# A written order of tasks for each engine, in place of priorities, in a fused attention and gated-MLP kernel

## The chip, the cores and the metric

The kernel runs on one NeuronCore of one Trainium2 chip. The metric is the device time of one execution in microseconds (us), lower is better.

## The reference

Everything is float32. Attention over 4 batches of 8 heads, 576 tokens, head dimension 64, with a threshold below the row maximum; its output goes through two feed-forward layers. The 2304 tokens have 512 features; the layers are 1024 and 2048 wide.

```python
def _attn_ref(q, k, v, tau):
    scores = scale * np.matmul(q, k.transpose(0, 1, 3, 2))
    thresh = np.max(scores, axis=-1, keepdims=True) - tau
    scores = np.where(scores >= thresh, scores, -1000000000.0)
    ...  # softmax
    return np.matmul(attn, v)

def _moe_ref(x, w_in, w_out, g_ln):
    h = x @ w_in
    solu = h * softmax(h)
    ...  # layer norm over the features, times g_ln
    return ln @ w_out

def _moe2_ref(x, w_in, w_out):
    h = x @ w_in
    return (h * tanh(softplus(h))) @ w_out
```

## The kernel before

The program is written as 5062 tasks, each one or a few instructions of one engine with its inputs and buffers. There are 1268 tasks for TensorE (PE), 1617 for VectorE (DVE), 1268 for ScalarE (ACT), 206 for GpSimd (POOL), 695 for SyncE (SP), which issues nearly all DMAs, and 8 without an engine of this count.

**Attention** goes by pairs of heads and blocks of 128 query rows. A score tile is made by `s_tile`: TensorE writes it to a PSUM buffer `st` (two) or `s3` (L810 for the first eight pairs, which use half the array's rows at a time; L817 for the others). VectorE takes its row maximum (TENSOR_REDUCE, L823), a short scalar op (L826) makes the threshold, ScalarE takes the exp (L824), and VectorE masks and sums it (SCALAR_TENSOR_TENSOR, L827); that last step releases the score buffer. `turn` transposes the result on TensorE (L854, L857, and L859 for the sums) into a PSUM bank `p_ta` or `p_mo`, ScalarE copies it out (L835), and `pv` multiplies it with V (L904). A score tile, a transpose and a product with V use the TensorE array in different modes.

**Weights** come as 64-bit numbers and are taken apart by `convert`: ScalarE (L651, L657), VectorE (L654 or L657, L659, L660, L662) and GpSimd (L665, L668) work on them between the other tasks; the mish layer's weights get seven sums and differences (L715, `add7`) and are stored to DRAM as `w2c`.

**The gated layer** (`moe_h` L961, `layer_norm` L968 to L991, `moe_t` L1010, `moe_y` L1031) follows each batch of attention, in tiles of 128 tokens.

**The mish layer** works in five visits of 768 tokens. `ff_in` and `ff_out` compute 2x2 blocks by seven products each; a product is six matmuls of 128x384 (L1129) into a PSUM bank `hoa` or `hob`. Weights are loaded into eight buffers A (L1159) and twenty buffers B (L1155), activations into y (L1145), partial sums into `acc` (L1234); results are stored from `acc` (L1278, L1283). ScalarE copies banks (L1179), takes mish (L1185) and splits numbers (L1215); VectorE adds and subtracts (L1182, L1189, L1217, L1253).

**The order.** Before the program is emitted, the `Plan` lays out all tasks in a planned time. At each step it looks, for each engine, at the tasks whose inputs are there, and takes the one with the best priority: the recorded number of the task (`KEYS`), less 250 times the planned wait. What it takes decides the order on each engine, which buffer a task gets, and where idle TensorE time early in the program is filled with dummy matmuls (L604). On the chip each engine runs its instructions in that order, each waiting for its semaphores. SP's DMAs are such a queue too.

Of the kernel before, what the change touches and what calls it, by code (L numbers as in the profile page):

```python
# [12 lines left out]
ALU = mybir.AluOpType  # L13
# [5 lines left out]
KEYS = (  # L19
    "bghl04mzxphMsWqgBaWiSh0xdrjfBgVsaTsRaL3isQkaTX8FbzLdamXiIot2iVxjpjrcGZkWcYPWYpa2OlRjcABeIUd3bb7qRL3WGfaQydyWiEEgyCgZYeth"  # L20
    "aE1aGZdM/iTbgiOjTZcmHbFhadHdpdiIUc9ye4uT98jVSc+/aq+gsha6wd0DgWpiCNchjboygDmdLZdNkgY8cAdZHKe7jaxobONeH5iRjeDlZ5td50dFoe2F"
    "fFTeLYbAdhOednab7dbhzdomcPaejxcnedvqZ7CcrchKeesXYREiK0goIfVAhtIb55a7FTRQjKQcWCcLxgGgcJabpidFpdDgfHjfBYZiPdUhbYMeHEYAjZTk"
    "bVNbzFd9CazYhlZZ0cV8Lfe7a/udINbI+gxObNvdSvhMvbrVgKObPmbXedyte+DcPcbrQe7oZ8ldb5aGjevKZkrb2Hea9ayicRadhda7rb7YeEAaoecSjZWB"
    "Z1wYUdb7/awTUNabW5a+cWmYbTYcBxWTCbZ+VPEY2vf2/g2eX58dZ+ZECfW7bf5ZJkYltZ7NZtoWqcbs6YI0fAfYUibevYpOYcMZm+gdKah8d+0a7HaJ2cNY"
    "aqeY8edcJep7Xv3dbFXhAYjeWPWYqNYYzYh2bmbasva/YU1/fvxXtNaZuYRdcO0bYWZgYYKBX8ycwPYW2bfsXSAWlQZycUEEdA6UzubigYLbYh0ZHrYsZZs2"
    "ZDxXm0acFYCDYCJXiEYwPaZXW5HX+0X7zYUZav2V2qfYcY4eZ+MXilaPGXoJYksWuHX6xYI7Ym4ZCZXm1ZR4YKDZxLXVQaJbXrIY8eWq5ZwSYXMbM4Wp6YZv"
    "W9LXPmXQMYQyXmTaVMX4cXf/Vl6WuLVxXZImc6nbNrYN8ZscUoQX2sWzWb7kZXEZDDWGEXYQVcGaFgWhhWOrWsCZ09UL+aEPXpQWMvWTOZkvU7QSr6Z9cWc4"
    "aXzYaIZLQWeAZZqXjlYYEanTZ7UVUZVcxWF+Xh/ZozUpWYxHbeLaMPaw6W3KWp0W3ZY6Jb2IWM1VNLWE7XZoWZxZN7WZNXluZo+WxpWZmWtLWE/XxeX+/Zy6"
    "YyEX49aESX2vYU5WJoZegV29WU1YxPdDuXIPUmgW1OUeTW++Vv3WhhYh2YkBZz8VGNU9DVlZXJjXU6VSAUlyUnFXhhYqSV5+Tn1UhTXYEWYJY2RXGAUwMVCM"
    "UobOm0VoMWmwZV/XbwU34YMGVkTVUwZWbXojUTSXNxT8PT7sUJBWbaU+qUn2UR/VTlWPbT5YVqOUz4UUCXLnSGMVdvWTVWXZTwQUbeROcYAfW35UY3SwNXaN"  # L30
    "S9uWZ1WuIVG4WdJTB7VkRVMXWw0VWlWVeVT/XEbSocTeXYBxVAgTGvS95WIVTq7SLKUe1UKTWiSVQ6RUCU7SWokVSyUEKTrjTpbVfTS07X88Ud7V1LVB8W/S"
    "TfBV7dTybU9HVFDTVIWjBVyOV1LTHMTo2TqTTknUtTUpPR0wUUZUb+UKPVsLULST8kWkbTLeVHdTw3VFrUOoUFBTZxTagV7JQ1mVaOUN2TUoT9zVjDSzeSzp"
    "TF1UeBTArUspTsOYo2TDxTQdPt4TvyV7tSf7TTtTUKUErS7GTAIUP/UmYU8qUGTTUiUBVS+jYM5TfTSgJS2FS7eUg0TsZUJVU/KR9GTwaS/YSlYT1wSiPT3B"
    "S00Sf5UFBTVnVYAVwbTdHSJwSdiTSqR6zT33S21S/2TlyRdBVJCQvlSiTS2CUkxPwZTV+SpUTDFT2jUPCTcJTxhTLTT3RSTXS+vT41SmJUEnT+BSZcSfyTU7"
    "Sk3VauVv9STaSxJSeITA1TjUT0uSmUSbpS1FSZvSmtVEBQnESs+S0sSpjTGYUVkIiFApIli/GmaPSVYMubTKZsFmzbhGckT+Y16Y0dpN5fvvfi6gDgm08XiV"
    "mzOWKLlk1cTUTcBOeEb3aii1b6NW5Vm70fkudpCbO4cY2fuhbUoisVYq3aBHfMFcRyhJFcO8fESmHqnvdkkklctX/3gjxc+hgdEbGGXWpVuMpimbEXfkei/0"
    "ozzw9prYJmDQknGbQ9YFPTHOdqycgqYlCc6lbwxjfVm65dwXXBWbsFhxRiADdJxaNycjYg72hfPoHPeNgXpBhvidFzchjgdpT2igmwv8ZVFZe00lAbTgbhys"
    "iedb0mkjyUrncVOqDGexagSLouki0QejZiFecNld2NhKjgZ3nliiAkjxLfJ1faKfn9VUmmsbeJudO+XgwcALbPfds6fSGcHRc6wdb7fuseQ1gr7aKmc6Uq3d"
    "cr3bk1nPAaSbbLkpNbe1wWsXcEdXMVg73cDGljXnuqYgFhFMfRmqyKdvBc8TfB6duniLLluZey2d0iesxhoPfSdcuSZuecNaV6Bm2glPsghGebzcmxnw2a9C"
    "ewMcroeJWkBoiVbbQJbE2gTzm88h6dfvOe8taVig6ScdFhjihihhg3hQ9fY/aePluWb+1ifmeCMaOLfnZefNh61bcpdEpfFac2Djy1gGUd0HnozlPThROXzv"  # L40
    "fC4jXqfcdf5vmpqfUQlorajToIcgu3doCav8dxljgDV9ggupghsjKcbJzj9NdW5jbdegtWOheu4e5/eMZh1naGFjRoVVKjPlZPbeRTbAieNbfHAif6c+Ne1R"
    "cVvcgKePPeGMZkVgDLisjSjWc1WeLlczVaPKmJibljcARhPHilKf4AfNAVMXfpvedBZTVchzbtzeVifT8hErfCAgNxfpFdakdTEg16n07emQcvOem1WXIh7F"
# [154 lines left out]
class Plan:  # L197
# [5 lines left out]


    COLD = 60.0
    RULE = 250.0, 3.0
    ISSUE, FIRST, LATENCY = 0.48, 0.95, 1.8
    LANES = 8
    LOAD = 1.3
# [28 lines left out]
    def place(self, choose, put, first):  # L238
# [7 lines left out]
        n = 0  # L246
# [1104 lines left out]
```

## Time and profile before

| what | value |
|---|---|
| median of 3 runs | 864.36 us (863.97 to 864.73) |
| profiled execution | 865.65 us, of it 863.9 us span from first to last instruction |
| TensorE busy | 842.5 us, 98% of the span |
| VectorE busy | 754.4 us, 87% |
| ScalarE busy | 626.7 us, 73% |
| GpSimd busy | 243.5 us, 28% |

A matmul's record reaches to its modelled end and overlaps the next one's, so TensorE's busy share is more than what it needs. Busy time counts neither waits nor DMA issue. The line numbers are those of the kernel before; from L606 on, a line of the changed kernel stands 15 lines earlier.

### The profile page before, as it was taken

The page shows a single profiled execution, that of the slowest core. Times are in us where ns is not written, and L with a number is a line of the kernel's source. Part 1 is how long each engine was busy: PE and PEld are TensorE (multiplying, and loading weights), DVE is VectorE, ACT ScalarE, POOL GpSimd, SP SyncE. Part 2 cuts the span into 40 slices and gives each one's busy share as a digit, 9 for nine tenths or more (in the row PEclk, how much of TensorE's full clock was granted, in tenths as well). Part 3 has the DMA queues.
Part 4 walks back from the last instruction along what each step waited for, and adds up shares of the span by engine and source line. Part 5 has one row for each costly group of instructions (what it writes and reads, how often), then busy time and mean ns, then how long its engine had stood idle before and what let it go on. Part 6 is the DMA issues. An engine that isn't in the chain of part 4 may idle for free.

```text
span 863.9 us, 16472 instructions
## 1 busy us (share of the span) xinstructions
PE 842.5 (98%) x5432; PEld 731.9 (85%) x5433; DVE 754.4 (87%) x1782; ACT 626.7 (73%) x1308; POOL 243.5 (28%) x210
## 2 busy tenths in 40 slices
PE   8889999999999999999999999999999999999998
PEld 4455666677788888797899999999999999989998
DVE  6997999899998999898867898889999998868786
ACT  5898898889898989867556778665757665646451
POOL 2346464533444434242222211011112210000000
PEclk9999999999999999999999999999999999999999
DMA  7666544323755374647988679999999999776733
GB/s 221 185 188 206 165 150 131 121 94 112 232 152 181 118 228 127 209 144 244 365 268 241 216 225 367 348 329 334 322 320 310 321 308 355 248 275 230 233 123 92
DMA packets 158197, 195.22 MB, mean 226 GB/s; under 512 B 15376, under 2 KB 115744, under 8 KB 158112
## 3 DMA queue, kind: packets, MB, share of 16 engines
q1 hardware_dynamic: 157680, 193.91, 69.0%
q8 instruction: 43, 0.70, 0.3%
q14 instruction: 42, 0.34, 0.1%
q10 hardware_dynamic: 432, 0.26, 0.1%
HBM read 142.94 MB, written 51.19 MB: 225 GB/s over the span
## 4 chain that ended last, share of the span: by engine, by line
PE 72%; DVE 5%; DMA 4%; ACT 3%; issue 1%; POOL 1%; SPq 0%; ACTq 0%; DVEq 0%; POOLq 0%
PE hoa L1129 27%; PE hob L1129 10%; PE p_mo L1031 7%; PE p_mo L961 6%; PE p_ta L904 5%; PE p_ta L854 4%; PE st L817 4%; PE hoa L1031 3%; PE hoa L961 2%; PE st L810 2%; DVE e L827 1%; PE p_mo L1010 1%; DVE m L823 1%; DMA A<-w2c 1%; DMA y<-yc 1%
## 5 line engine op out<-in xcount | busy, mean ns | idle before, releaser
L827 DVE SCALAR_TENSOR_TENSOR e<-st,m,e 128x576 f32<-128x576 f32 x139 | 111.7, 813 | 14.3 <-ACT e L824 11.2
L1129 PE MATMUL hoa<-y,A 128*128 128x384 f32 x594 | 115.5, 336 | 1.7 <-DMA A<-w2c 1.5
L824 ACT ACTIVATE e<-st,m 128x576 f32<-128x576 f32 x139 | 101.9, 743 | 18.2 <-DVE m L823 16.8
L823 DVE TENSOR_REDUCE m<-st 128x1 f32<-128x576 f32 x139 | 102.6, 751 | 9.6 <-PE st L810 6.2
L1129 PE MATMUL hoa<-gh,B 128*128 128x384 f32 x492 | 105.7, 335 | 0.8 <-ACT B L1156 0.5
L1129 PEld LDWEIGHTS hoa<-y,A 128*128 128x128 f32 x594 | 103.4, 188 | 2.9 <-ACT gf L1185 1.8
L1215 ACT ACTIVATE gh<-gf 128x384 fp32r<-128x384 f32 x168 | 81.7, 518 | 28.9 <-PE hob L1129 8.9
L1217 DVE TENSOR_TENSOR gl<-gf,gh 128x384 fp32r<-128x384 f32 x168 | 87.0, 558 | 2.7 <-PE hob L1129 1.9
L1129 PEld LDWEIGHTS hoa<-gh,B 128*128 128x128 f32 x492 | 86.7, 188 | 2.1 <-ACT B L1156 0.8
L854 PE MATMUL p_ta<-ident,e 128*128 128x128 f32 x576 | 83.5, 277 | 4.3 <-DVE m L826 1.3
L1189 POOL TENSOR_TENSOR gf<-gf 128x384 f32<-128x384 f32 x24 | 24.5, 1019 | 218.6 <-DVE gf L1189 154.9
L854 PEld LDWEIGHTS p_ta<-ident,e 128*128 128x128 f32 x576 | 64.8, 140 | 23.3 <-issue 3.8
L665 POOL TENSOR_TENSOR ws<-cf,cl 128x512 uint32<-128x512 uint32 x32 | 41.4, 1292 | 128.0 <-DVE cf L662 20.3
L1253 DVE TENSOR_TENSOR acc<-acc,hoa 128x384 f32<-128x384 f32 x107 | 57.2, 548 | 9.4 <-PE hoa L1129 7.3
L1031 PE MATMUL p_mo<-LH,W2H 128*128 128x256 f32 x216 | 64.3, 298 | 0.0
L1185 ACT ACTIVATE gf<-gf 128x384 f32<-128x384 f32 x72 | 37.6, 523 | 36.2 <-DVE gf L1182 35.8
L1129 PE MATMUL hoa<-gl,B 128*128 128x384 f32 x246 | 62.6, 335 | 0.0
L1031 PE MATMUL p_mo<-LL,W2H 128*128 128x256 f32 x216 | 61.1, 283 | 0.0
L1031 PE MATMUL p_mo<-LH,W2L 128*128 128x256 f32 x216 | 61.0, 282 | 0.0
L835 ACT ACTIVATE ey<-p_ta 128x512 f32<-128x512 f32 x80 | 46.2, 603 | 6.0 <-PE p_ta L854 5.4
L810 PE MATMUL st<-Kst,Qhh 64*128 64x256 f32 (+3 forms) x300 | 48.9, 445 | 1.4 <-DVE e L827 1.2
L1156 ACT ACTIVATE B<-B 128x256 fp32r<-128x256 f32 x112 | 41.4, 409 | 11.5 <-DMA B<-w2c 11.4
(147 smaller groups left out, 2242.3 us busy)
## 6 DMA issues: line engine op xcount, KB each, us to landing
A<-w2c SPq DMA_DIRECT2D x140, 256.0 KB, 4.2
y<-yc SPq DMA_DIRECT2D x28, 768.0 KB, 6.8
w2c<-ws SPq DMA_DIRECT2D x32, 448.0 KB, 5.2
B<-w2c SPq DMA_DIRECT2D x112, 128.0 KB, 5.9
cr<-w_in SPq DMA_DIRECT2D x32, 256.0 KB, 4.5
cr<-w_out SPq DMA_DIRECT2D x32, 256.0 KB, 4.0
yc<-yh SPq DMA_DIRECT2D x9, 896.0 KB, 4.6
yc<-ys SPq DMA_DIRECT2D x9, 896.0 KB, 5.8
```

The source lines that it names most:

```text
L810: TE.matmul(flat()[r, c:c + w], f(qh.tile[a, i * 128 + r.start:i * 128 + r.stop]), f(ks.tile[a, k:k + w]), start=True, stop=True)
L823: t = add("DVE", dve(S), lambda: V.tensor_reduce(m.tile[:, 2:3], x(), AX.XY, ALU.max, negate=True), [t], [m], [st])
L824: a = add("ACT", act(S, True) + 0.1, lambda: SC.activation(et(), x(), ACTF.Exp, bias=m.tile[:, 2:3]), [t], [e] if h == 0 else (), [st, m, ...
L827: t = add("DVE", dve(S) + 0.06, lambda: V.scalar_tensor_tensor(et(), x(), m.tile[:, 1:2], et(), ALU.is_ge, ALU.mult, accum_out=sr.tile[:, ...
L835: x.append(add("ACT", act(n, True), lambda: SC.activation(dst(x[0]), src(), ACTF.Copy), [dep], (), [tp, x[0]]))
L854: TE.transpose(tp.tile[:, k * 128:(k + 1) * 128], e.tile[:, o:o + 128], ident)
L961: TE.matmul(h.tile, l.tile[:, kt], r[:, kt, j * 512:(j + 1) * 512], start=(kt == 0 and x == 0), stop=(kt == KD - 1 and x == 2))
L1031: TE.matmul(y.tile[:, :PN], l[:, k, cs], r.tile[:, k], start=(k == 0 and x == 0), stop=(k == KF - 1 and x == 2))
L1129: TE.matmul(x.tile[:, :TH], l, r, start=new and n == 0, stop=stop and n == len(steps) - 1, skip_group_check=True)
L1215: a = add("ACT", act(TH), lambda h=h, x=x: SC.activation(h.tile, full(x), ACTF.Copy), [first], [h], [h, x])
L1217: out[c] = h, l, a, add(e, cost(TH), lambda h=h, l=l, x=x, eng=eng: eng.tensor_tensor(l.tile, full(x), f(h.tile), ALU.subtract), [a, *deps ...
L1253: d = add("DVE", dve(TH), lambda: V.tensor_tensor(to(), to(), fr(), ALU.add), deps + [CO.get((v, e, i, t))], use=[ac, x])
```

## The change

The table of priorities is replaced by a table of places, `TURN`: for each task, its place in the order of its engine. The planner then never chooses. It keeps one list for each engine and takes from it the next task, at the planned time at which its inputs, buffers and bank are there. Planned start-up times change with it: SP starts at 0.73, the first two K loads are counted on SP, and four short VectorE operations are given other planned durations. No instruction is added, removed or given other data.

```diff
-KEYS = (
+TURN = (
-    "bghl04mzxphMsWqgBaWiSh0xdrjfBgVsaTsRaL3isQkaTX8FbzLdamXiIot2iVxjpjrcGZkWcYPWYpa2OlRjcABeIUd3bb7qRL3WGfaQydyWiEEgyCgZYeth"
+    "AAJAALAAOAAGAAMAAEAAjAAZAAfAAiAAmAAqAA0AA4AAKABLAA1AA/ABEABIABQABcABiAAuABlABuACFACTAClADCADSADcABsADbACqADMADXADkADoAD3"
...
-    RULE = 250.0, 3.0
...
-    def place(self, choose, put, first):
...
-                    picked[e] = choose(e, ready[e])
...
+    def lines(self):
...
+            a, b, c = (place[k] for k in TURN[z:z + 3])
+            t.key = a * 4096 + b * 64 + c
+        return {e: sorted((t for t in self.tasks if t.eng == e), key=lambda t: -t.key) for e in self.ORDER if e != "-"}
+
+    def place(self, first, put, choose):
+
+        line, free, picked, stale = self.lines(), [t for t in first if t.eng == "-"], {}, set(self.ORDER)
+        for n in range(len(self.tasks)):
+            for e in stale:
+                if e == "-":
+                    t = min(free, key=lambda t: t.at, default=None)
+                else:
+                    t = line[e][-1] if line[e] and not line[e][-1].left else None
+                picked[e] = (1.0e9, self.ORDER[e], None) if t is None else (choose(e, t), self.ORDER[e], t)
+            b, _, t = min(picked.values(), key=lambda x: x[:2])
...
-                k = wait * (at - now) - t.key if at > now else -t.key
...
-    plan = Plan({"ACT": 2.5, "DVE": 3.9, "POOL": 5.6, "SP": 1.5, "PE": 4.6}, "exp", load_table, tc)
+    plan = Plan({"ACT": 2.5, "DVE": 3.9, "POOL": 5.6, "SP": 0.73, "PE": 4.6}, "exp", load_table, tc)
...
-            t = add(*("-", 3.6 + 0.5 * n) if first else ("SP", dma(512 * KW, 4 * KW)), lambda: D(f(ks.tile[:, :KW]), k1[n // H_, n % H_]), new=[ks], order=k_in)
+            t = add("SP", dma(512 * KW, 4 * KW) + 0.5 * (first and not n), lambda: D(f(ks.tile[:, :KW]), k1[n // H_, n % H_]), new=[ks], order=k_in)
...
-        b = add("DVE", 0.08, lambda: V.tensor_scalar(m.tile[:, 1:2], m.tile[:, 2:3], -1.0, nt8, ALU.mult, ALU.add), [t, k_c], use=[m])
+        b = add("DVE", 0.115, lambda: V.tensor_scalar(m.tile[:, 1:2], m.tile[:, 2:3], -1.0, nt8, ALU.mult, ALU.add), [t, k_c], use=[m])
```

What it does to the instructions is shown at three places.

The first is VectorE's queue in the attention, at the softmax tiles that ran from 62.8 to 69.4 us in the kernel before: `m` holds a tile's row maximum, `e` its exponentials, `cf` and `cz` belong to `convert`, `sr` are the row sums. Before:

```order
L823 TENSOR_REDUCE m<-st 128x1
L662 SCALAR_TENSOR_TENSOR cf<-cr,cz 128x512
L847 TENSOR_SCALAR sr<-sr 128x5
L848 RECIPROCAL sr<-sr 128x5
L826 TENSOR_SCALAR m<-m,cs 128x1
L827 SCALAR_TENSOR_TENSOR e,sr<-st,m,e 128x576
L823 TENSOR_REDUCE m<-st 128x1
L826 TENSOR_SCALAR m<-m,cs 128x1
L823 TENSOR_REDUCE m<-st 128x1
L827 SCALAR_TENSOR_TENSOR e,sr<-st,m,e 128x576
```

After the change (L808 is L823, L811 is L826, L812 is L827, L644 is L659):

```order
L808 TENSOR_REDUCE m<-st 128x1
L811 TENSOR_SCALAR m<-m,cs 128x1
L808 TENSOR_REDUCE m<-st 128x1
L812 SCALAR_TENSOR_TENSOR e,sr<-st,m,e 128x576
L811 TENSOR_SCALAR m<-m,cs 128x1
L808 TENSOR_REDUCE m<-st 128x1
L832 TENSOR_SCALAR sr<-sr 128x5
L644 TENSOR_SCALAR cz<-cz 128x512
L833 RECIPROCAL sr<-sr 128x5
L812 SCALAR_TENSOR_TENSOR e,sr<-st,m,e 128x576
```

The tile whose reduce is the seventh row before has it in the third row now, and its SCALAR_TENSOR_TENSOR, the last row in both, has six rows between where it had two.

The second is TensorE's queue in the attention, around the transpose that started at 112.73 us: `p_ta` and `p_mo` are PSUM banks, `e` a masked exponential, `so` a tile of the gated layer. Before:

```order
L857 MATMUL p_ta_1545<-ident,e 128x128
L810 MATMUL st<-Kst,Qhh 128x256
L810 MATMUL st<-Kst,Qhh 128x320
L854 MATMUL p_ta_1558<-ident,e 128x128 x4
L854 MATMUL p_ta_1566<-ident,e 128x128 x4
L1010 MATMUL p_mo_1572<-ident,so 128x128 x4
L1010 MATMUL p_mo_1582<-ident,so 128x128 x4
```

After the change (L842 is L857, L795 is L810, L839 is L854, L995 is L1010):

```order
L795 MATMUL st<-Kst,Qhh 128x256
L795 MATMUL st<-Kst,Qhh 128x320
L839 MATMUL p_ta_1549<-ident,e 128x128 x4
L839 MATMUL p_ta_1558<-ident,e 128x128 x4
L995 MATMUL p_mo_1565<-ident,so 128x128 x4
L995 MATMUL p_mo_1576<-ident,so 128x128 x4
L842 MATMUL p_ta_1584<-ident,e 128x128
```

The single transpose of the first row before (L857) is the last row now; the score tile, the two transposes of four and the two of the gated layer stand ahead of it.

The third is TensorE's queue in the mish layer, around 754 to 761 us: a row with A is a whole product of `ff_in`, a row with B the first of the six of a product of `ff_out`, the other five being left out. The first row is the last reader of the buffer into which the A tile of the last row is loaded. Before:

```order
L1129 MATMUL hob_9846<-y7x,A_9798 128x384 x6
L1129 MATMUL hoa_10102<-y_9709,A_10016 128x384 x6
L1129 MATMUL hob_10114<-gh,B_9735 128x384
...
L1129 MATMUL hob_10129<-gh,B_9735 128x384
...
L1129 MATMUL hob_10114<-gh,B_9875 128x384
...
L1129 MATMUL hob_10129<-gh,B_9875 128x384
...
L1129 MATMUL hoa_10162<-y_9535,A_10109 128x384 x6
```

After the change:

```order
L1114 MATMUL hoa_10100<-y_9589,A_9918 128x384 x6
L1114 MATMUL hoa_10112<-y_8402,A_10028 128x384 x6
L1114 MATMUL hoa_10131<-gh,B_9652 128x384
...
L1114 MATMUL hob_10047<-gh,B_9816 128x384
...
L1114 MATMUL hoa_10151<-gh,B_9452 128x384
...
L1114 MATMUL hob_10167<-gh,B_9452 128x384
...
L1114 MATMUL hoa_9931<-y_9511,A_9909 128x384 x6
L1114 MATMUL hoa_10191<-y_10002,A_10028 128x384 x6
L1114 MATMUL hoa_9931<-y7x,A_9951 128x384 x6
L1114 MATMUL hoa_10151<-gh,B_9660 128x384
...
L1114 MATMUL hoa_10229<-y_9589,A_10119 128x384 x6
```

Between the product that frees the buffer and the one that reads the new tile stand five products before, and nine now.

## Rows read from the trace of the kernel before

**Rows 1.** Page, busy us, share of the span and instructions of each engine

```profile
PE 842.5 (98%) x5432; PEld 731.9 (85%) x5433; DVE 754.4 (87%) x1782; ACT 626.7 (73%) x1308; POOL 243.5 (28%) x210
```

**Rows 2.** Busy times in stretches of the span; columns as in the first row

```profile
core 0: us, PE busy (x) PEld busy (x) DVE busy (x) ACT busy (x) POOL busy (x), PEclk, DMA share, GB/s
...
10.00:230.00 220.00, 207.16 (x1444) 140.34 (x1445) 199.11 (x496) 192.42 (x386) 104.93 (x97) 1.00 0.52 164
230.00:520.00 290.00, 289.41 (x2033) 254.41 (x2033) 250.03 (x606) 226.19 (x448) 97.62 (x73) 1.00 0.66 207
520.00:856.00 336.00, 333.47 (x1907) 329.54 (x1906) 297.23 (x661) 205.37 (x473) 40.25 (x36) 1.00 0.85 285
```

**Rows 3.** Waits of VectorE, 0 to 230 us: total us, times, longest

```profile
DVE m L823 <- PE st L810: 6.2, 13, 2.4
DVE e L827 <- ACT e L824: 4.3, 8, 1.1
...
DVE cz L659 <- ACT cz L657: 1.7, 3, 1.1
DVE ln L985 <- ACT em L984: 1.4, 3, 0.9
```

**Rows 4.** Waits of TensorE, 230 us to the end

```profile
PE hoa L1129 <- DMA A<-w2c: 1.5, 1, 1.5
PE hoa L1129 <- ACT B L1156: 0.5, 1, 0.5
```

**Rows 5.** VectorE in order of time, 62 to 69.5 us: start, us, instruction, [wait]

```profile
64.28 0.16 DVE L847 TENSOR_SCALAR sr<-sr 128x5 f32<-128x5 f32 x1
64.47 0.19 DVE L848 RECIPROCAL sr<-sr 128x5 f32<-128x5 f32 x1
...
66.32 0.75 DVE L823 TENSOR_REDUCE m<-st 128x1 f32<-128x576 f32 x1
67.11 0.22 DVE L826 TENSOR_SCALAR m<-m,cs 128x1 f32<-128x1 f32 x1
67.30 0.76 DVE L823 TENSOR_REDUCE m<-st 128x1 f32<-128x576 f32 x1
68.64 0.82 DVE L827 SCALAR_TENSOR_TENSOR e<-st,m,e 128x576 f32<-128x576 f32 x1 [0.58 <-ACT e L824]
...
69.39 0.42 DVE L659 TENSOR_SCALAR cz<-cz 128x512 f32<-128x512 f32 x1
```

**Rows 6.** TensorE in order of time, 107.5 to 115 us

```profile
112.73 0.30 PE L857 MATMUL p_ta<-ident,e 128*128 128x128 f32 x1 [1.30 <-DVE ln L990]
112.96 0.81 PE L810 MATMUL st<-Kst,Qhh 64*128 64x256 f32 x4
113.70 1.09 PE L854 MATMUL p_ta<-ident,e 128*128 128x128 f32 x8
114.63 0.60 PE L1010 MATMUL p_mo<-ident,so 128*128 128x128 f32 x4
```

**Rows 7.** Chain that ended last, 744 to 812 us: start, us, what

```profile
753.16 1.05 PE hob L1129 x6
...
754.23 6.51 DMA A<-w2c
...
760.87 2.33 PE hoa L1129 x12
...
771.89 1.04 PE hoa L1129 x6
```

**Rows 8.** TensorE in order of time, 20.5 to 24.5 and 43 to 52 us

```profile
21.53 0.80 PE L810 MATMUL st<-Kst,Qhh 64*128 64x320 f32 x4
22.07 0.70 PE L810 MATMUL s<-Kst,Qhh 64*128 64x320 f32 x4
22.70 0.66 PE L854 MATMUL p_ta<-ident,e 128*128 128x128 f32 x4
23.19 0.33 PE L857 MATMUL p_ta<-ident,e 128*128 128x128 f32 x1
...
44.73 0.80 PE L810 MATMUL st<-Kst,Qhh 64*128 64x320 f32 x4
45.47 1.09 PE L854 MATMUL p_ta<-ident,e 128*128 128x128 f32 x8
```

**Rows 9.** Page, costliest groups: busy us, mean ns, idle before

```profile
L824 ACT ACTIVATE e<-st,m 128x576 f32<-128x576 f32 x139 | 101.9, 743 | 18.2 <-DVE m L823 16.8
```

More of the change, by code (lines that the diff above doesn't have):

```diff
@@ L262 @@
     ORDER = {e: k for k, e in enumerate(("PE", "DVE", "ACT", "POOL", "SP", "-"))}
[L264 removed]
+    def lines(self):
         digits = "ABCDEFGHIJKLMNOPQRSTUVWXYZabcdefghijklmnopqrstuvwxyz0123456789+/"
         place = {c: k for k, c in enumerate(digits)}
[L268 to L272 removed]
+        for z, t in zip(range(0, len(TURN), 3), self.tasks):
+            a, b, c = (place[k] for k in TURN[z:z + 3])
+            t.key = a * 4096 + b * 64 + c
+        return {e: sorted((t for t in self.tasks if t.eng == e), key=lambda t: -t.key) for e in self.ORDER if e != "-"}
@@ L274, in forward @@
+    def forward(self):
         free, done, table = dict(self.start), [], self.table
@@ L282, in forward, with choose, put @@
             t.left = len(t.need)
-        def choose(e, c):
-            now, best = free.get(e, 0.0), None
+        def choose(e, t):
+            now, at = free.get(e, 0.0), t.at
+            for x in t.takes:
+                at = max(at, min(x.buf.free, default=1.0e9))
             if e == "PE":
-                gap = {id(g): min((bank[b][0] for b in g if bank[b]), default=1.0e9) for g in self.groups}
-            for t in c:
-                at, late = t.at, 0.0
-                for x in t.takes:
-                    at = max(at, min(x.buf.free, default=1.0e9))
-                if e == "PE":
-                    if t.bank:
-                        at = max(at, gap[id(t.bank.buf.banks)])
-                    if t.mode != mode:
-                        at = max(at, now + self.CHANGE[mode][t.mode])
-                elif t.port:
-                    at = max(at, port, hand if e == "POOL" else 0.0)
-                k = wait * (at - now) - t.key if at > now else -t.key
-                if t.table and t.table != table:
-                    k, late = k + avoid, self.LOAD
-                if best is None or (k, t.at) < best[:2]:
-                    best = k, t.at, max(now + late, at), t
-            return best[2], self.ORDER[e], best[3]
-        def put(b, t, open_, stale):
+                if t.bank:
+                    at = max(at, min((bank[b][0] for b in t.bank.buf.banks if bank[b]), default=1.0e9))
+                if t.mode != mode:
+                    at = max(at, now + self.CHANGE[mode][t.mode])
+            elif t.port:
+                at = max(at, port, hand if e == "POOL" else 0.0)
+            return max(now + (self.LOAD if t.table not in (None, table) else 0.0), at)
+        def put(b, t, loose, stale):
             nonlocal port, hand, dma, table, mode
@@ L357, in forward @@
             t.at = 0.0
-        return done if self.place(choose, put, first) else None
+        self.place(first, put, choose)
+        return done
     def idle(self, order):
@@ L764, in operands @@
                 w = c.stop - c.start
-                q = add(*("-", 3.8 + 0.7 * n) if first and not z else ("SP", dma(512 * w, 4 * w)), lambda c=c, go=SC.dma_start if first and not z else D: go(f(qh.tile[:, c]), qq[n // H_, n % H_][:, c]), [], [qh] * (z == 0), [qh], order=OPS[n][0][1:] + k_in * (first and not z))
+                q = add(*("-", 3.8) if first and not z else ("SP", dma(512 * w, 4 * w)), lambda c=c, go=SC.dma_start if first and not z else D: go(f(qh.tile[:, c]), qq[n // H_, n % H_][:, c]), [], [qh] * (z == 0), [qh], order=OPS[n][0][1:] + k_in * (first and not z))
                 if first and not z:
```

294 lines of the change are left out of this document (137 added, 157 removed).

## The prediction

> **What bounds the kernel now.** I read first the busy times of the page, then the same by stretches, then who waited for whom on the two engines that could be the limit, and only then single places in order of time.
>
> The page gives TensorE 842.5 us of 863.9 [rows 1], but matmuls overlap in that row, so it cannot say where time is lost. The stretches can [rows 2]; the granted clock is 1.00 in each, so no term below hangs on the clock. From 10 to 230 us (attention, with the first tiles of the gated layer) VectorE (DVE) is busy 199.1 of 220 us, and idle 20.9; TensorE is idle 12.8 even by its generous count. From 230 to 520 us TensorE is idle 0.6 of 290, and from 520 to 856 us (the mish layer) 2.5 of 336. So there are two regimes. Up to about 230 us VectorE's work sets the pace, and only its gaps can be closed. After that TensorE sets it: what the first regime gives back arrives at the end one for one, and besides it only 3.1 us can be had.
>
> What ends VectorE's gaps up to 230 us [rows 3]: it waits for ScalarE 7.4 us in the three largest groups (4.3 for the exp L824, 1.7 for the convert's Abs L657, 1.4 for L984) and for TensorE's score tiles 6.2 us, 2.4 of them at once. After 230 us TensorE waits 1.5 us for one weight load and 0.5 us for a split weight [rows 4]; smaller waits are left out.
>
> **The change, part by part.** It replaces the rule by which a planner picks the next instruction by a written order for each engine. Counted in the two orders, the 5062 tasks are the same, with the same arithmetic, but for two start-up loads that the planner now counts on SP; a TensorE task moves by 3 places on average, a VectorE task by 6. So nothing is added or removed in work, and only gaps can come or go.
>
> *A, the stretch to 230 us.* I counted what stands ahead of TensorE's 371st task, a transpose that waits for VectorE at 230 us: 415 VectorE tasks before, 413 now. The two that moved behind are one step L654 (priced by its like L659, 0.42 us) and one L715 (no row here; at most the same), so 0.4 to 0.8 us, taken as 0.7. The rest of VectorE's work up to there is the same, so the gaps decide.
>
> A gap of the commonest kind stands at 68.64 us [rows 5]: the reduce of a softmax tile ends at 67.07, its scalar_tensor_tensor L827 starts 1.57 us later, and in between there was only 0.97 us of other work, a scalar op and the next tile's reduce; the 0.58 us left over is the wait for the exp. The exp itself takes 743 ns [rows 9]; the other 0.8 us are hand-offs and ScalarE's queue. In the new order the same tile has the previous tile's L827 (0.82), the scalar op (0.2), the next reduce (0.76), a sum (0.16), a shift (0.42) and a reciprocal (0.19) in between, 2.55 us in all, so this wait goes if the exp is not later. Counted so over the 95 tiles whose L827 starts before 240 us, the tiles with under 1.5 us of such cover fall from 69 to 52, a quarter. I take a quarter of the 7.4 us: 1.9. Bounds: nothing, if ScalarE's queue only gets later by as much, and all 7.4.
>
> For the waits on TensorE I find less. The VectorE work between the release of a score buffer and the reduce of the next tile in it is not larger now: of 92 pairs, 24 had under 1.2 us, and 26 have. Only for the longest wait, 2.4 us, does the count give 1.2 us more cover. I take those 1.2; bounds 0 and 6.2. The place shown at 112.73 us is of the same sort on the other engine [rows 6]: TensorE stood 1.30 us before a single transpose L857, with a score tile, two transposes and two transposes L1010 queued behind it, which then ran from 112.96 to 115.2 without a wait. In the new order these stand ahead of it, so up to 2.3 us of ready work fills that gap. It is no term of its own, since VectorE sets the pace there; it counts by the score tile coming sooner.
>
> A comes to 0.7 + 1.9 + 1.2 = 3.8 us.
>
> *B, TensorE's changes of mode.* The new order has more of them: 147 where there were 128, all 19 more ahead of the 371st task. Their price is seen where score tiles stand between transposes [rows 8]: from one score tile to the next it is 0.54 us (21.53 to 22.07), from a score tile to a transpose 0.63 (22.07 to 22.70) and 0.74 (44.73 to 45.47), so leaving costs 0.09 to 0.20. 19 of them cost 1.7 to 3.8 us. They lie in the stretch where TensorE has 12.8 us idle beside a busier VectorE, which is the work that hides them: I take 0, and 3.8 with that cover gone. The Trainium skill, page "TensorEngine Tiling (Array Packing)", section "Key Properties", says that changing the tiling mode drains TensorE. That speaks against this change. The rows agree that a change costs something; as a full drain of one transpose, 0.33 us, the 19 would be 6.3 us by it, and by the rows 3.8 at most.
>
> *C, the mish layer.* A product of six matmuls takes 1.04 us here [rows 7]. The wait of 1.5 us at 760.87 us is for the weight tile A, whose load started at 754.23 and took 6.51. SP could issue it only when the product freed its buffer at about 754, and five products stand between that one and the first that reads the new tile: 5.2 us. In the new order there are nine, 9.4 us, against 6.5 us of load and the issue ahead of it. So the whole wait goes: 1.6 us with its tail. Over all loads of this layer, seven had five products or fewer of such lead, and none has now; the least goes from four to six. Likewise the pairs in which a bank is copied out with only one product between its writer and the next that writes it fall from 40 to 27; I take 0.5 us of the 0.9 us that is left for all that. C is 2.1 us; bounds 0 and 2.5. Against it stands that the last y load has 8 products of lead where it had 11; a miss there costs about 1.5 us.
>
> *D, the start.* SP sends the gated layer's first weights earlier and two late operands later; TensorE's first score tiles wait for the same loads as before. 0, bounds -1 and +1. In the stretch from 230 to 520 us TensorE is full, and changes between products of one mode show no cost: 0.
>
> *The sum.* 3.8 + 0 + 2.1 + 0 = 5.9 us. Made against the profiled execution, 865.65 becomes 859.75; that execution is 1.29 us above the median of the runs shown, 864.36, from which the forecast is 858.5.
>
> **The rivals.**
>
> *The gaps only move.* Each wait removed comes back at the next instruction of the same queue, because ScalarE, busy 192.4 of the 220 us [rows 2], cannot deliver sooner. For it: the cover of the score buffers did not grow, and VectorE's work ahead of 230 us is the same within 0.7 us. Against it: ScalarE's 27.6 us of idle time there are more than VectorE's 20.9, and the long transposes and weight waits have ready work put ahead of them by count. A would be 0.7, C half: 864.36 - 1.7 = 862.7 at best, 864.4 if C is eaten by new waits. I call it 864.
>
> *Slower: the mode changes are not hidden.* If VectorE waits for score tiles (6.2 us in rows 3) just where TensorE pays for the added changes, their 3.8 us fall on the path. With A and C as forecast the result is still 2.1 us faster; slower needs A's waits to stay as well: 864.36 + 3.8 - 0.7 - 1.6 = 865.9. It decides from the point where A gives less than 1.7 us. The page named under B would have it so, each drain being paid in full.
>
> *More than forecast.* Half of VectorE's 20.9 us goes, since small gaps that no row names shrink with the same cover, and C is whole: 10.5 + 2.5 = 13, thus 851.4. For it: the cover grew in most of the waits that I counted, not only in the quarter taken. Against it: those are the places where the old order did badly, and others take their turn.
>
> **How the numbers follow.** The forecast, faster by 3 to 9 us, has 0.56; more than that 0.19; the moved gaps 0.13; slower 0.12. 0.2%, 1.7 us, is about what a measurement of this kernel tells from no change: faster 0.76, same 0.13, slower 0.11, since a hundredth of the moved gaps ends beyond that bound on the fast side, and as much of the slower rival within it. The range leaves a tenth at either side: it reaches into the larger gain, 852.5, and to no gain at all with half the added changes paid, 865.0. The forecast's own range is 855.5 to 861.5.
>
> **What the profile after would show.** VectorE's idle time from 10 to 230 us falls from 20.9 to about 17, the waits for the exp by a quarter, and the transpose at 230 us comes about 4 us sooner. TensorE's wait for tile A is gone and no other load has taken its place. TensorE's count of score tiles and transposes is the same, but they stand in shorter runs. The prediction is wrong if VectorE's idle time is the same (then the gaps moved), if TensorE waits for loads in the mish layer under new names (C), or if VectorE waits longer for score tiles (B).

## The result, and the profile after

The changed kernel takes 853.97 us (853.69 to 854.52), the kernel before on the same chip 864.15: a ratio of 0.9876 (0.9855 to 0.9897). By the medians it is 10.2 us faster where 5.9 were forecast; that is above the forecast's own 3 to 9 us and inside the whole range, which ends at 852.5. (The changed kernel's first four runs gave 0.9889, 0.9870 to 0.9909; the profiled one of them ran at a granted clock of 0.79 and is left out. All rows of after are of a later execution, 854.06 us, span 852.3, clock 0.997.)

Busy times by stretches, to be held against [rows 2]; columns as there:

```profile
core 0: us, PE busy (x) PEld busy (x) DVE busy (x) ACT busy (x) POOL busy (x), PEclk, DMA share, GB/s
10.00:230.00 220.00, 216.81 (x1511) 145.05 (x1509) 202.06 (x521) 196.18 (x398) 105.76 (x97) 1.00 0.55 167
```

From 10 to 230 us VectorE is idle 17.9 us where it was 20.9, nearly the 17 forecast. But TensorE is idle 3.2 where it was 12.8, and it has done 67 matmuls more by then, seven of them dummies. (Of the planner's dummies there are two more in all, so "No instruction is added" in the part on the change is not exact.) The transpose that started at 230.28 us before, on which the forecast of A hung, now starts at 223.30, 6.98 us sooner. The stretches up to that same transpose, before and then after:

```profile
0.00:230.28 230.28, 215.75 (x1474) 144.25 (x1476) 204.22 (x514) 195.38 (x390) 105.86 (x102) 1.00 0.53 166
```

```profile
0.00:223.30 223.30, 216.76 (x1476) 143.62 (x1476) 199.14 (x512) 193.06 (x389) 106.25 (x102) 0.99 0.55 167
```

TensorE is idle 14.53 us up to it before and 6.54 after, 7.99 less, and busy 1.01 more: together the 6.98. VectorE is idle 1.90 us less and busy 5.08 less, for two instructions fewer.

Who waited for whom, VectorE first, to be held against [rows 3] (total us, times, longest):

```profile
DVE m L808 <- PE st L795: 7.1, 15, 1.1
DVE e L812 <- ACT e L809: 4.6, 13, 1.2
...
DVE Qhh L754 <- DMA Qhh<-qq: 2.3, 2, 2.1
DVE ln L962 <- ACT so L953: 2.3, 2, 1.4
```

The wait for the exp did not fall by a quarter; it went from 4.3 to 4.6 us. The wait for score tiles grew from 6.2 to 7.1, which the prediction had named as a sign of being wrong on B. What went is TensorE's own. These are the five largest of its thirteen groups before, 10 to 230 us:

```profile
PE p_ta L857 <- ACT ex L835: 2.2, 3, 1.4
PE st L817 <- DVE e L827: 1.6, 3, 0.8
PE p_ta L857 <- DVE m L826: 1.5, 2, 0.8
PE p_ta L857 <- DVE ln L990: 1.3, 1, 1.3
PE p_ta L854 <- DVE m L826: 1.3, 1, 1.3
```

and the largest three of seven after:

```profile
PE st L795 <- DVE e L812: 0.7, 3, 0.3
PE p_ta L839 <- ACT ey L820: 0.5, 1, 0.5
PE st L795 <- POOL Qhh L754: 0.4, 1, 0.4
```

The single transpose that had waited 1.30 us [rows 6] stands behind the others and does not wait:

```profile
110.86 1.04 PE L995 MATMUL p_mo<-ident,so 128*128 128x128 f32 x8
111.74 0.27 PE L842 MATMUL p_ta<-ident,e 128*128 128x128 f32 x1
```

In the mish layer the same 1390 matmuls took 244.80 us before (first row) and take 240.70 now (second), TensorE without a gap:

```profile
609.10:853.90 244.80, 242.89 (x1390) 240.07 (x1389) 215.69 (x483) 144.13 (x329) 29.72 (x27) 1.00 0.80 264
```

```profile
601.60:842.30 240.70, 240.70 (x1390) 240.54 (x1389) 213.11 (x481) 139.32 (x326) 29.02 (x26) 1.00 0.82 272
```

Of [rows 4] nothing is left, and no other wait is listed there after 520 us. The chain that ended last, by engine, on the page of before and then of after:

```profile
PE 72%; DVE 5%; DMA 4%; ACT 3%; issue 1%; POOL 1%; SPq 0%; ACTq 0%; DVEq 0%; POOLq 0%
```

```profile
PE 90%; DVE 3%; ACT 3%; DMA 2%; issue 1%; POOL 1%; ACTq 0%; SPq 0%; DVEq 0%; POOLq 0%
```

### The profile page after: what moved, and what is told of

Same layout as the page of the kernel before. It is cut to its first block, busy times and chain, and to the rows that moved or that the text cites. A ratio compares the mean times of both kernels' runs of the same rounds, so it can differ in the third digit from the quotient of the medians.

```text
span 978.0 us, 16403 instructions
## 1 busy us (share of the span) xinstructions
PE 970.4 (99%) x5434; PEld 811.9 (83%) x5434; DVE 749.1 (77%) x1782; ACT 628.9 (64%) x1308; POOL 244.4 (25%) x210
## 4 chain that ended last, share of the span: by engine, by line
PE 98%; DMA 1%; DVE 0%; ACT 0%; issue 0%; ACTq 0%; DVEq 0%
PE hoa L1114 30%; PE p_ta L889 11%; PE p_mo L946 10%; PE p_mo L1016 9%; PE p_ta L839 9%; PE hob L1114 8%; PE st L802 5%; PE st L795 5%; PE hoa L1016 3%; PE hoa L946 2%; PE p_mo L995 2%; PE p_ta L842 1%; DMA Qhh<-qq 1%; PE p_ta L589 0%; PE hoa L995 0%; PE s L795 0%
## 5 line engine op out<-in xcount | busy, mean ns | idle before, releaser
L808 DVE TENSOR_REDUCE m<-st 128x1 f32<-128x576 f32 x139 | 103.2, 755 | 68.7 <-PE st L802 37.1
L1114 PE MATMUL hoa<-y,A 128*128 128x384 f32 x654 | 137.3, 356 | 0.0
L812 DVE SCALAR_TENSOR_TENSOR e<-st,m,e 128x576 f32<-128x576 f32 x139 | 112.9, 815 | 20.1 <-ACT e L809 13.8
L1114 PEld LDWEIGHTS hoa<-y,A 128*128 128x128 f32 x654 | 121.9, 192 | 2.1 <-DVE gf L1167 0.4
L1114 PE MATMUL hoa<-gh,B 128*128 128x384 f32 x492 | 112.6, 352 | 0.0
L839 PE MATMUL p_ta<-ident,e 128*128 128x128 f32 x576 | 102.0, 318 | 0.7 <-ACT ey L820 0.4
L839 PEld LDWEIGHTS p_ta<-ident,e 128*128 128x128 f32 x576 | 76.1, 151 | 27.0 <-issue 5.6
L1202 DVE TENSOR_TENSOR gl<-gf,gh 128x384 fp32r<-128x384 f32 x168 | 93.3, 568 | 3.6 <-PE hob L1114 1.1
L1016 PE MATMUL p_mo<-LH,W2H 128*128 128x256 f32 x216 | 71.3, 330 | 0.0
L795 PE MATMUL st<-Kst,Qhh 64*128 64x256 f32 (+3 forms) x300 | 57.6, 503 | 1.9 <-DVE Qhh L754 1.6
L946 PE MATMUL p_mo<-W1H,XH 128*128 128x512 f32 x116 | 58.6, 505 | 0.0
L1164 ACT ACTIVATE gf<-hoa 128x384 f32<-128x384 f32 x60 | 29.3, 488 | 44.7 <-PE hoa L1114 35.6
```

Source lines behind the costliest of these rows:

```text
L795: TE.matmul(flat()[r, c:c + w], f(qh.tile[a, i * 128 + r.start:i * 128 + r.stop]), f(ks.tile[a, k:k + w]), start=True, stop=True)
L808: t = add("DVE", dve(S), lambda: V.tensor_reduce(m.tile[:, 2:3], x(), AX.XY, ALU.max, negate=True), [t], [m], [st])
L812: t = add("DVE", dve(S) + 0.06, lambda: V.scalar_tensor_tensor(et(), x(), m.tile[:, 1:2], et(), ALU.is_ge, ALU.mult, accum_out=sr.tile[:, ...
L839: TE.transpose(tp.tile[:, k * 128:(k + 1) * 128], e.tile[:, o:o + 128], ident)
L946: TE.matmul(h.tile, l.tile[:, kt], r[:, kt, j * 512:(j + 1) * 512], start=(kt == 0 and x == 0), stop=(kt == KD - 1 and x == 2))
L1016: TE.matmul(y.tile[:, :PN], l[:, k, cs], r.tile[:, k], start=(k == 0 and x == 0), stop=(k == KF - 1 and x == 2))
```

## The experiments

All kernels use the changed planner and differ in the table of places, or in one added instruction. "Old" and "new" are the orders of before and after; line numbers are those of the changed kernel. Ratios are to the kernel before on the same chip, with 95% intervals.

| run | us, median | ratio |
|---|---|---|
| new order | 853.97 | 0.9876 (0.9855 to 0.9897) |
| old order | 865.08 | 1.0000 (0.9984 to 1.0015) |
| new, then old | 857.52 | 0.9918 (0.9900 to 0.9936) |
| old, then new | 864.32 | 1.0003 (0.9988 to 1.0018) |
| old, TensorE's moved | 875.44 | 1.0130 (1.0108 to 1.0153) |
| old, VectorE's apart | 866.18 | 1.0022 (1.0009 to 1.0035) |
| old, both | 879.99 | 1.0196 (1.0166 to 1.0226) |
| new, VectorE's together | 891.73 | 1.0325 (1.0301 to 1.0349) |
| new, lead of three | 857.99 | 0.9935 (0.9911 to 0.9959) |
| new, more modes | 860.36 | 0.9947 (0.9927 to 0.9967) |
| old, dose on VectorE | 865.15 | 1.0007 (0.9997 to 1.0018) |
| old, dose on TensorE | 870.51 | 1.0079 (1.0055 to 1.0104) |

**Where the gain lies: the order or what goes with it, early or late.** The first run is the changed kernel itself.

> The changed kernel itself, for a profile at the full clock and a narrower interval. Its first runs stood 9.6 us below the kernel before, against 5.9 forecast. Theory S (the forecast's terms are right in kind, A too small): about 854.6 us; VectorE's idle time from 10 to 230 us falls from 20.9 to about 14, TensorE's work of the stretch after comes about 7 us sooner, and the wait for tile A is gone (2 to 2.5 us). Theory L (A as forecast, the rest in TensorE's later stretches): VectorE's idle time falls to about 17 only, and TensorE gains some 5 us after 230 us, though only 3.1 us of idle time stood there before; then matmuls themselves must run closer together.

Theory S gave the time and the 7 us by which TensorE's later work comes sooner; theory L gave VectorE's idle time, 17.9 us where S had 14.

The second has the old order in the new planner; the next two splice the orders at TensorE's 380th task:

```diff
-turn = new
+turn = old                                                   # old order
+turn = upto(new, pe=380) + [t for t in old if t not in it]   # new, then old
+turn = upto(old, pe=380) + [t for t in new if t not in it]   # old, then new
```

> The order of before on all five engines, written as places and emitted by the changed kernel's planner, with its new planned durations. Theory: the order alone carries the change, so this stands within 0.2% of the kernel before, 864 us. Rival: a part of the gain comes from what goes with the order (dummy matmuls at other places, SP's planned start, other banks and buffers taken in the same order); then it lies between 864 and 855, and the difference to 864 is that part.

> The new order up to TensorE's 380th task (about 232 us) on all engines, the old order behind it. Theory S: it keeps term A whole, near -7 us, thus about 857.5. Theory L: it keeps the forecast's A, -3.8, thus about 860.5. A splice can add a little loss at the seam, under 1 us.

> The opposite splice: the old order up to TensorE's 380th task, the new one behind it. Theory S: it keeps C alone, -2 to -2.5 us, thus about 862. Theory L: it keeps some -6 us, thus about 858. If the two splices add up to the whole gain, the two stretches are independent.

The old order in the new planner is the kernel before again, so the order carries the whole change. The first splice keeps 6.6 of the 10.2 us, which speaks for theory S; the new order behind it is worth the other 3.6. The opposite splice gains nothing that can be measured, where S expected 2 to 2.5 us. Its trace, held against that of the old order over the same matmuls of TensorE, says why: it is 0.2 us ahead in front of the seam, 1.1 behind at 550 us, and 1.2 ahead at the end. At the seam TensorE waits 1.6 us for a score buffer's release where the old order waits 0.8. In the mish layer the new order then gains 2.3 us. Counted in the same way over "new, then old", it gains 2.6 us in that layer behind the new early part. So the late order is worth nearly the same behind either early part, as far as one execution of each tells; what the seam costs hides it in the medians.

**Is it TensorE's waits?** In the old order, 20 of TensorE's tasks were moved behind what looked ready. The first:

```diff
 L839 MATMUL p_ta_250<-ident,e 128x128 x4
-L842 MATMUL p_ta_259<-ident,e 128x128
 L795 MATMUL st<-Kst,Qhh 128x320
 L795 MATMUL st<-Kst,Qhh 128x256 x2
 L795 MATMUL st<-Kst,Qhh 128x320
+L842 MATMUL p_ta_274<-ident,e 128x128
```

> The old order, with 20 tasks of TensorE's queue between 12 and 222 us moved back by one to three places, each behind work that was ready. These are the places where the next matmul started 0.3 to 1.9 us later than the pitch of the matmul ahead of it, 14.6 us in all; the other engines keep the old order. Theory Q (a task that waits at the head of TensorE's queue holds score tiles back, and the new order removed just these waits, 17.4 to 5.6 us): half or more of the early gain, 857.5 to 861 us. Theory V (the forecast's: VectorE sets the pace up to 230 us, and such a wait is no term of its own): under 1 us, 863 to 864.

Neither theory said slower, and it is 11 us slower. The score tiles brought forward were not ready. TensorE's score tiles in the first half of attention, 10 to 230 us, in this run (busy, mean ns | idle before):

```profile
L795 PE MATMUL st<-Kst,Qhh 64*128 64x320 f32 (+3 forms) x292 | 48.0, 446 | 7.4 <-DVE e L812 2.4 <-POOL XL L935 1.4 <-POOL xo L908 1.2
```

The same row of the kernel before:

```profile
L810 PE MATMUL st<-Kst,Qhh 64*128 64x320 f32 (+3 forms) x292 | 46.9, 440 | 1.4 <-DVE e L827 1.2
```

Of the 7.4 us the row puts 2.4 down to L812, the step that releases a score buffer, and 2.6 to steps of GpSimd, the engine that makes Qhh, an input of the tile. My choice had looked only at whether the inputs were there in the old order's trace, and not at whether the buffer was free. A part of the 11 us is the clock's: behind waits of 1.21, 0.69 and 0.88 us between 23 and 31 us TensorE's granted clock is 0.50 (1.2 GHz) from 31 to 37 us, where the old order's is 1.00; that is up to 3 us. So this run does not tell Q from V; it shows that a wait on TensorE's queue is not gone because work is put ahead of it.

**Is it VectorE's neighbours?** In the traces VectorE pays for an instruction directly behind the one whose result it reads, and no view calls that a wait. In the old order such neighbours were set apart (first diff), in the new one brought together (second):

```diff
 L808 TENSOR_REDUCE m<-st 128x1
-L811 TENSOR_SCALAR m<-m,cs 128x1
 L832 TENSOR_SCALAR sr<-sr 128x4
+L811 TENSOR_SCALAR m<-m,cs 128x1
```

```diff
 L644 TENSOR_SCALAR cz<-cz 128x512
+L645 TENSOR_SCALAR cz<-cz 128x512
+L647 SCALAR_TENSOR_TENSOR cf<-cr,cz 128x512
 L833 RECIPROCAL sr<-sr 128x4
 L812 SCALAR_TENSOR_TENSOR e,sr<-st,m,e 128x576
 L808 TENSOR_REDUCE m<-st 128x1
-L645 TENSOR_SCALAR cz<-cz 128x512
```

> The old order, with 44 neighbours swapped in VectorE's queue up to 232 us, so that an instruction does not stand directly behind the one whose result it reads: such neighbours fall from 100 to 40, where the new order has 53. In the traces the step from a reduce to the next instruction is 0.79 us when that one reads its result and 0.67 us when it does not, and 0.46 to 0.34 for a 128x512 step: 0.12 us each, none of it shown as a wait. Theory N (this hidden 0.12 us is what the new order saves inside VectorE's busy time): 60 x 0.12 = 7.2 us of VectorE time, of which 2 to 5 us reach the end, 859 to 862. Rival W (only waits for other engines count, as in the forecast; the exps come later by one instruction): 863.5 to 865.

> Both sets of moves in the old order. If Q and N both hold and the two engines share the pace: the largest gain of the three, 856 to 859, about the splice's 857.5. If one engine alone sets the pace, no more than the better of the two single ones.

> The new order, with 108 of VectorE's instructions up to 226 us moved forward, directly behind the one whose result they read (threshold behind its reduce, the second and third integer step of a weight conversion behind the first): neighbours of this kind go from 53 to 140. The exps can start sooner, TensorE's queue is unchanged. Theory N: 87 x 0.12 = 10.4 us more VectorE time, of which 4 to 10 us reach the end, 858 to 864. Rival W: the same as the new order or faster by the sooner exps, 852 to 855.

The price itself is there: in the run set apart, in order of time, the instruction behind a reduce starts 0.67 us after it when it reads something else and 0.79 when it reads its result.

```profile
64.80 0.76 DVE L808 TENSOR_REDUCE m<-st 128x1 f32<-128x576 f32 x1
65.47 1.03 DVE L647 SCALAR_TENSOR_TENSOR cf<-cr,cz 128x512 uint32<-128x512 uint32 x1
...
68.30 0.75 DVE L808 TENSOR_REDUCE m<-st 128x1 f32<-128x576 f32 x1
69.09 0.21 DVE L811 TENSOR_SCALAR m<-m,cs 128x1 f32<-128x1 f32 x1
```

But the kernel with 60 fewer such pairs is 0.2% slower, and with TensorE's moves on top 2.0% slower: theory N falls, as far as the time is concerned. (That VectorE is busy 5.08 us less up to the transpose of the result is near what 47 fewer pairs, 100 less 53, would give at 0.12 us. The doses below show that this does not reach the end.) The run that brings them together is 38 us slower than the new order, nearly four times what N could explain. Its waits of VectorE, 10 to 230 us:

```profile
DVE m L808 <- PE st L795: 18.4, 19, 3.0
DVE cf L647 <- POOL W2L L665: 7.5, 4, 2.2
...
DVE cf L647 <- POOL W1L L665: 3.5, 2, 2.0
```

The third step of a conversion, moved up, now waits 11.0 us at the head of VectorE's queue for a buffer that GpSimd holds, and the softmax tiles wait behind it. That is a blocked queue, not N, and the run says nothing on N. Its granted clock in that stretch is 0.96, where the new order has 1.00, so that up to 0.04 x 220 = 8.8 us of the 38 can be the clock's.

**The lead of the A tile (term C).** One product was moved forward in the new order, to three products behind the one that frees its buffer:

```diff
+L1114 MATMUL hoa_10166<-y_9589,A_10119 128x384 x6
...
 L1114 MATMUL hoa_9931<-y_9511,A_9909 128x384 x6
 L1114 MATMUL hoa_9931<-y7x,A_9951 128x384 x6
...
-L1114 MATMUL hoa_10229<-y_9589,A_10119 128x384 x6
```

> The new order, with one product of the mish layer moved forward by six places in TensorE's queue, so that three products instead of nine stand between the one that frees the buffer and the one that reads the new tile A there (the place at 755 us). Theory C (the lead in products against the load's time decides): three products are 3.1 us against 5.1 to 6.5 us of load, so TensorE waits 2 to 3.5 us there and the kernel ends 2 to 3.5 us later, 856 to 857.5. Rival: the wait is made up behind it, since the products that were passed over stand there and the loads gain time; then under 1 us.

The only large wait of TensorE after 230 us in that run, and the load in the chain that ended last:

```profile
PE hoa L1114 <- DMA A<-w2c: 2.7, 1, 2.7
```

```profile
748.17 5.68 DMA A<-w2c
...
753.99 1.83 PE hoa L1114 x6
```

5.68 us of load less 3.1 of lead, with 0.14 between the landing and the start, give the 2.7. But the wait is not all that the edit costs. The two products behind it, in order of time, and the stretch in which they lie:

```profile
753.99 1.83 PE L1114 MATMUL hoa<-y,A 128*128 128x384 f32 x6 [2.72 <-DMA A<-w2c]
755.62 1.48 PE L1114 MATMUL hob<-gh,B 128*128 128x384 f32 x4
756.90 0.84 PE L1114 MATMUL hob<-gl,B 128*128 128x384 f32 x2
757.54 1.03 PE L1114 MATMUL hoa<-gh,B 128*128 128x384 f32 x4
```

```profile
754.00:758.00 4.00, 4.00 (x14) 4.00 (x15) 0.22 (x1) 0.00 (x0) 0.00 (x0) 0.57 0.80 300
```

They take 3.55 us (753.99 to 757.54), where two products take 2.08: behind the wait the granted clock is 0.57 for these 4 us, most of it at the lower level of 1.2 GHz. In the new order, without the wait, it is 1.00 there. So the wait costs 1.5 us more than its own 2.7. Held against the new order's trace over the same matmuls, this execution is 1.60 us behind ahead of the place and 6.55 behind it and up to the end: 4.95 us, of which 2.7 are the wait, 1.5 the clock, and 0.7 not settled. By the medians it is 4.0 us, by the ratios 5.1. Nothing is made up behind the place: C's mechanism holds, and its price lacked the clock.

The 1.60 us are there at 20 us already, where the edit changes nothing. The first score tile's four matmuls take 1.44 us in this execution and 0.81 in the new order's, and nine dummies from 10 us on 3.77 against 2.61. What slowed them the rows do not tell, for the granted clock is 1.00 there.

**The changes of mode (term B).** Ten swaps of neighbours in TensorE's queue add 17 changes to the new order. One of them:

```diff
 L844 MATMUL p_ta_1139<-ident,sr 5x128
-L842 MATMUL p_ta_1143<-ident,e 128x128
 L795 MATMUL st<-Kst,Qhh 128x320
 L795 MATMUL st<-Kst,Qhh 128x256
+L842 MATMUL p_ta_1155<-ident,e 128x128
 L795 MATMUL st<-Kst,Qhh 128x256
 L795 MATMUL st<-Kst,Qhh 128x320
```

> The new order, with ten pairs of neighbours swapped in TensorE's queue between 22 and 177 us, each in a run of two tasks of one kind before two of another, where the input of the task moved forward was ready: A A B B becomes A B A B. It adds 17 changes of mode ahead of the 371st task (133 to 150), nearly as many as the new order added to the old. By the rows, 0.1 to 0.23 us each, 3.6 us in all. Theory B0 (forecast: hidden beside VectorE): under 0.8 us, 854 to 855. Theory B1 (TensorE's queue sets the pace there now, so they are paid): 2 to 3.6 us more, 856 to 857.6.

It costs 0.9947 - 0.9876 = 0.0071, or 6.1 us: B0 falls. The place of the diff in the new order, and with the swap:

```profile
77.93 0.27 PE L844 MATMUL p_ta<-ident,sr 128*5 128x128 f32 x1
78.04 0.32 PE L842 MATMUL p_ta<-ident,e 128*128 128x128 f32 x1
78.29 1.24 PE L795 MATMUL st<-Kst,Qhh 64*128 64x320 f32 x8
79.46 2.37 PE L889 MATMUL p_ta<-ey,V 128*64 128x320 f32 x16
```

```profile
80.12 0.27 PE L844 MATMUL p_ta<-ident,sr 128*5 128x128 f32 x1
80.32 0.80 PE L795 MATMUL st<-Kst,Qhh 64*128 64x320 f32 x4
81.05 0.33 PE L842 MATMUL p_ta<-ident,e 128*128 128x128 f32 x1
81.31 0.81 PE L795 MATMUL st<-Kst,Qhh 64*128 64x256 f32 x4
82.05 2.37 PE L889 MATMUL p_ta<-ey,V 128*64 128x320 f32 x16
```

From the transpose of the sums (L844) to the product with V it is 1.53 us (77.93 to 79.46) and 1.93 (80.12 to 82.05): two more changes, 0.40 us, at the upper end of what the rows of before priced [rows 8]. Over the same matmuls of the two traces the ten places add 0.13 to 0.69 us each and 3.1 in all. Between the places another 1.0 us is lost: TensorE's waits for the masked exponential (L812) go from 0.7 to 1.7 us. This execution is 1.60 us behind ahead of the first swap, as the lead test's was and with the same slow matmuls up to 14 us; it is 5.66 behind at the last swap (178 us) and 5.7 at the end. So 4.1 us are the swaps', and all of it arrives. That is far from B0's 0.8, and a little more than B1's 3.6.

**Which engine sets the pace before 230 us.** The last two runs add some 6 us of work to VectorE, and 10 to TensorE, in the old order:

```diff
 V.scalar_tensor_tensor(et(), x(), m.tile[:, 1:2], et(), ALU.is_ge, ALU.mult, accum_out=sr.tile[:, k:k + 1])
+if p < PX:
+    V.tensor_scalar(dose, on, 0.125, None, ALU.mult)
```

```diff
 TE.transpose(tp.tile[:, k * 128:(k + 1) * 128], e.tile[:, o:o + 128], ident)
+if k == 0 and p < PX:
+    TE.transpose(tp.tile[:, :128], e.tile[:, o:o + 128], ident)
```

> The old order, with 108 extra instructions in VectorE's queue, one behind each masked exponential (SCALAR_TENSOR_TENSOR) of the first ten pairs of heads: a tensor_scalar on a 128x1 scratch tile that nobody waits for. By the rows such a short one takes 0.08 to 0.13 us, so 9 to 12 us of added VectorE work, nearly all before 230 us. Theory V (the forecast's: up to 230 us VectorE sets the pace, TensorE has room): 8 us or more reach the end, 872 us or more. Theory K (neither engine's work alone sets the pace; each has short waits for the other that take a part of it): a half, 868 to 870. Theory T (TensorE's queue sets it): under 3 us.

> The old order, with 90 extra matmuls in TensorE's queue, the first of each four transposes of the first ten pairs done twice, with the same data into the same place: 0.11 us each, 9.8 us in all, no change of mode, nearly all before 230 us. Theory V: it lies beside VectorE's work in TensorE's idle time (12.8 us there), under 2 us reach the end, 864 to 866. Theory K: a half, 868 to 870. Theory T: 8 us or more.

The doses in the traces, VectorE's and TensorE's (count: duration, first and last start):

```profile
L817 DVE TENSOR_SCALAR dose<-cs x90: 142/148/153, 9.0 to 232.6; 128x1 f32<-128x1 f32 x90
```

```profile
L842 PE MATMUL p_ta<-ident,e x90: 271/273/273, 8.8 to 235.8; 128*128 128x128 f32 x90
```

There are 90 of each, where VectorE's expectation had 108. A short instruction's record overlaps the next one's:

```profile
64.42 0.15 DVE L817 TENSOR_SCALAR dose<-cs 128x1 f32<-128x1 f32 x1
64.49 0.75 DVE L810 TENSOR_REDUCE m<-st 128x1 f32<-128x576 f32 x1
```

It takes 0.07 us of the queue, so VectorE got 90 x 0.07 = 6.3 us, less than the 9 to 12 expected, and TensorE 90 x 0.11 = 9.9. Of VectorE's 6.3 us 0.07% arrived, 0.6 us (-0.3 to 1.6); of TensorE's 9.9 us 0.79%, 6.8 us (4.8 to 9.0). In the traces, over the same matmuls from 22 to 241 us, VectorE's dose makes 1.3 us of delay more than the old order has, and TensorE's 5.0. Theory V falls on both. K falls on VectorE's, where half would be 3 us, and T on TensorE's, where it had 8 us or more; 870.5 lies just above K's range. So none of the three fits both. But a half to two thirds of TensorE's added work arrives, and a tenth to a fifth of VectorE's: in the old order, the kernel before, TensorE's queue is much nearer to setting the pace, though not alone.

## Why the prediction was right, and which step of it failed

**The step that failed** is the sentence "Up to about 230 us VectorE's work sets the pace, and only its gaps can be closed". The doses show it wrong for the kernel before: of what VectorE does more four fifths or more are hidden, of what TensorE does more a half to two thirds are paid. The rows leaned that way: TensorE was busy 207.16 of 220 us and VectorE 199.11 [rows 2]. I set the larger number aside because matmul records overlap. But VectorE's overlap as well, as the dose shows (0.15 us of record, 0.07 of queue), so neither count was the better one.

**A** had the right sign, and neither its size nor its mechanism. Forecast: 3.8 us, half of it from shorter waits for the exp. Measured: 6.6 us by the splice, and the waits for the exp did not shrink. I had written of TensorE's 1.30 us wait that it "is no term of its own, since VectorE sets the pace there"; by the traces such waits were the term. Up to the transpose on which A hung TensorE's idle time fell by 7.99 us, its busy time rose by 1.01, and the transpose comes 6.98 sooner. By experiment only two things are shown, that added work on TensorE is paid in good part and that the early order is worth 6.6 us. Removing the waits by themselves was tried and put other waits in their place, so that they alone make the gain is argued, not shown.

**B** was taken as hidden, at 0. In the new order it is not: 17 changes more cost 4.1 us in the trace, 6.1 by the ratios, and TensorE's queue has no cover for them. The price in the rows was right, 0.18 us for one (3.1 for 17); the cover was not there, and waits come on top, 0.24 to 0.36 for one in all. What the change's own 19 cost no run prices by itself; it is in the 6.6 us of A. The Trainium skill, page "TensorEngine Tiling (Array Packing)", section "Key Properties", by which a change of mode drains the array, is borne out in kind; the 0.18 for one by itself is a little over half of the 0.33 that I had worked out for a full drain.

**C** is right in its size rather than in its parts. Forecast were 2.1 us, 1.6 of them for tile A and 0.5 for all the rest. Measured are 3.6 behind the new early part by the medians, of which 2.6 lie in the mish layer by the traces, and 2.3 in the opposite splice. The wait for tile A went, no other load took its place, and the lead test brought such a wait back, with its price. But "new, then old" keeps the old five products of lead, and no wait for a tile A is listed there either. So in that execution the early part alone took the wait away, without the longer lead, and between 740 and 763 us of that run the new order gains only 0.5 us more. The rest is spread over several places of 0.2 to 0.8 us, which I had priced together at 0.5. The ceiling of 2.5 us, read from idle time, was wrong too. A matmul that starts late inside the modelled end of the one ahead leaves no idle time: before 520 to 856 us had 2.5 us of it, yet the same 1390 matmuls shrank by 4.1 us from 609 us on alone, 2.2 of it in busy time (242.89 to 240.70).

**D**: a new wait of 2.1 us for the first queries stands at 7 us, and by TensorE's 30th task it is made up (30.1 us before, 30.0 after, counted in the traces). 0 was right.

**The rivals.** "The gaps only move" is what VectorE's own waits did, and what each hand-made move did; for the whole order it was wrong. "Slower" had its mechanism right, mode changes that are paid, and lost because the waits that went were larger than its price. "More than forecast" was nearer the time (851.4) than the forecast, by the wrong engine's idle time: 10.2 us is more than the 9 at which that rival began. The time lies within the stated range only because the range reached into this rival, and because errors had opposite signs: the idle time that A won was twice its forecast, and B, taken at nothing, took a part of it back. That is luck more than mechanism.

## What to carry to other kernels

Where two engines are both over 90% busy, don't choose the pacing one by busy time: add some microseconds of harmless work to each in turn and see what arrives. And an order is one thing across all engines: putting a task ahead because its inputs were ready in the old trace is not enough, since its buffer may not be free, and then it blocks everything behind it. A load's lead, counted in products against its duration, gave the wait within 0.2 us once the duration was known; it was 6.51 us before and 5.68 in the lead test.

## What the runs showed of the hardware

A VectorE instruction directly behind the one whose result it reads started 0.12 us later than one that reads something else (0.79 against 0.67 us behind a 128x576 reduce), and this stands in busy time. By the records the dependent one starts 0.04 us after the reduce's end (68.30 + 0.75, then 69.09), the other 0.09 before it (64.80 + 0.76, then 65.47). The Trainium skill, page "VectorE: DVE Perf Modes", section "The DRAIN you can't avoid", says both that a semaphore after each of a row of copies costs nothing extra, since the next waits for the pipe to empty anyway, and that an instruction that is not held starts earlier; the rows agree with the second and add its size here. Taking 60 such pairs away gained no time, since in that order VectorE's work hardly reached the end.

TensorE's granted clock was 1.00 over the mish layer of the new order and 0.57 from 754 to 758 us of the lead test, behind a wait of 2.72 us; behind the wait of 1.5 us of the kernel before it stayed at 1.00. Such a wait cost more than its own length, 1.5 us here.
